# VectorE waits for the GpSimd instruction that precedes it on the shared port

## The chip, the cores and the metric

The kernel runs on one core of a Trainium2 chip. A core has five engines that work side by side[...]: TensorE (PE in the profile, its weight loads PEld) multiplies matrices, ScalarE (ACT) evaluates functions, VectorE (DVE) and GpSimd (POOL) do elementwise work, and SyncE (SP) issues transfers. The time is the device time of one execution in microseconds. Before the change it is 772.55 us, the median of three runs between 772.16 and 772.81.

## The reference

A gate mixes two branches over one input x of 2048 rows and 512 columns, all in bf16:

```
g = sigmoid((x * gate_w).sum(-1))
out = g * A(x) + (1 - g) * B(x)
```

A is attention with 32 heads of width 16: `softmax(q k^T / 4) v`, then a projection `wo`. The scores are 32 x 2048 x 2048 numbers, and each needs an exponential. B is a mixer: a layer norm, a projection `w1` with GELU, a shift of four column groups by one or two rows, a projection `w2` and a residual; then a layer norm, `w3` (to 1792 columns) with GELU, and `w4`, with a residual.

## The kernel before, in words

**Attention in rounds.** There are 32 rounds: four column blocks of 512 queries, by four groups of eight heads, by two halves of a group. A round takes 64 score tiles of 128 keys by 512 queries. TensorE computes a tile (L842) from `kT` and `q`. An exponential turns it into weights, and TensorE multiplies these with `V` and adds into the PSUM bank `acc` (L1017). `V` has a column of ones, so the sum of the weights comes with it.

**Two ways to the exponential.** Most tiles go to ScalarE in pairs: `PA<-psA`, 128x1024, L922. The others go to VectorE. There a trick on the bits of a 16-bit number stands for the exponential: a multiply and an add make an integer whose bits, read as bf16, approximate the power (L948, `PD<-ring`, one tile of 512 from a PSUM bank called `ring`). Two tiles make a pair of 1024 columns. Three shifted copies of the pair are then made by adding a constant to the integers (`close_pair`, L984 on VectorE, L986 on GpSimd, all of them `PD<-PD`, from SBUF to SBUF in 16 bits), and the four versions are added up by four products with `V`, or with `V2`, a scaled copy. VectorE makes the first copy, and mostly the second; GpSimd makes the third, and at times the second too. Pairs marked `alone` have all copies made by VectorE.

**Other work.** VectorE also casts the projections out of PSUM (L578, L601, L618, L733, L765), makes the masked copies of q (L603), scales `V` (L623), normalises rows for the layer norms (L688, L695), scales x by the gate (L753), empties `acc` at the end of each round (L1033), and multiplies the reciprocals of the sums with the gate (L1041). GpSimd also multiplies the emptied `acc` with the broadcast reciprocals (L1050) and computes the inverse deviations of the layer norm (L684, L686).

**Who sets the order.** No scheduler runs on the chip. When the kernel is built, a planner (`Sim`) plays through the whole execution with a cost for each job, and decides at each moment which job an engine takes next. The instructions are then emitted in the order of the planned start times, and each engine works its own list strictly in that order. Dependencies through data become semaphore waits.

**The shared port.** VectorE and GpSimd share a port to SBUF. The planner knows this: a job marked `port=True` (all of GpSimd's, and of VectorE's those that read SBUF in the ways concerned: L603, L623, L688, L695, L753, L984, L1041) starts in the plan only when `self.lock` has passed, that is, when the last such job of either engine is planned to be over (`try_engine`). The plan so has the port's jobs of both engines in one row. `in_port_order` makes the chip keep to that row, as far as it adds waits for it. Before the change it adds them on one side: a GpSimd instruction waits for the last VectorE port instruction that precedes it in the row (`last_port`). A VectorE port instruction has no such wait; it starts when its data and its buffers are there, and what happens on the port then is left to the hardware.

Of the kernel before, what the change touches and what calls it, by code (L numbers as in the profile page):

```python
# [89 lines left out]
class Sim:  # L90
# [50 lines left out]
    def in_port_order(self, e, fn):  # L141

        def issue():
            inst = fn()
            if e == "DVE":
                self.last_port = inst
            elif inst is not None and self.last_port is not None:
                self.tc.add_manual_dep(inst.ins, self.last_port.ins.name, mybir.DependencyInfo(
                    mybir.DependencyClass.Sync, mybir.DependencyReason.DATA), reason="port")
        return issue  # L150

    def finish_job(self, job):
# [93 lines left out]
def kernel(  # L246
# [89 lines left out]
    def slots(name, n, shape, dt=BF16, where=const):  # L336
        return [where.tile(shape, dt, name=f"{name}{i}") for i in range(n)]
# [38 lines left out]
    sim = Sim({  # L376
        **{f"psA{w}{n}": slots(f"psA{n}", 1, [P, 512 * w], F32, ps) for n, w in enumerate(WIDTHS)},
        "ring": sim_ring,
        "PA": slots("PA", NPA, [P, 512 * max(WIDTHS)]),
        "token": list(range((NPD - 1) // 3)),  # L380
        "PD": slots("PD", NPD, [P, 1024], U16),
        "w": slots("w", NW, [P, KT, D]),
        "xnT": slots("xnT", 2, [P, KT, 512]),
        "xn": slots("xn", 2, [P, D]),
# [11 lines left out]
        "rr": slots("rr", 3, [4, 512], F32, dpool),  # L396
    })
    sim.tc = tc
    sim.last_port = None

    def dve(hold, deps, fn, **kw):
        return sim.add(Job("DVE", hold, 280.0, deps, fn, **kw))
# [971 lines left out]
```

The softmax here doesn't subtract the row's maximum and nothing guards it: scores larger than these inputs give would overflow.

## Time and profile before

| what | value |
|---|---|
| time, median of 3 | 772.55 us |
| span of the profiled execution | 770.4 us |
| TensorE busy | 758.7 us, 98% |
| ScalarE busy | 739.7 us, 96% |
| VectorE busy | 725.2 us, 94%, 1575 instructions |
| GpSimd busy | 335.2 us, 44%, 332 instructions |
| one shifted copy on VectorE (L984, 128x1024) | 429 ns mean, 286 to 1262 ns, x579 |
| one shifted copy on GpSimd (L986, 128x1024) | 1048 ns mean, 1041 to 1215 ns, x270 |
| one tile's bits on VectorE (L948, 128x512) | 680 ns mean, x565 |

Busy time is the union of the stretches in which an engine executes something. A wait on a semaphore is not busy time: the engine is idle, and the profile names who released it. A wait inside an instruction that has started is different: the instruction simply takes longer, and shows only in its duration. Consecutive VectorE instructions overlap a little in the trace[...]. The ends of matmuls are modelled, so a busy TensorE is not TensorE at its peak.

### The profile page before, as it was taken

To read this page: it belongs to the slowest core of one execution; us is meant where nothing else is said; L and a number is where in the kernel's file an instruction comes from. 1 tells how busy PE (TensorE), PEld (TensorE's weight loads), DVE (VectorE), ACT (ScalarE), POOL (GpSimd) and SP (SyncE) were. 2 spreads that over 40 slices of the span, in tenths; PEclk is the share of its full clock that TensorE was granted. 3 is DMA by queue.
4 is the path that set the end of the run, shared out by engine and by line. 5 is a ranking of instruction groups with operands and counts; after the bars stand their busy time and mean duration, and the time that the engine had idled before them with its cause. 6 is when DMAs were issued, how large, how long until landed. Compare 5 with 4: busy or idle time off the path is not lost.

```text
span 770.4 us, 23725 instructions
## 1 busy us (share of the span) xinstructions
PE 758.7 (98%) x9588; PEld 227.8 (30%) x9588; DVE 725.2 (94%) x1575; ACT 739.7 (96%) x767; POOL 335.2 (44%) x332
## 2 busy tenths in 40 slices
PE   9999999999999999999999999999999999999997
PEld 5333322223222222233232224222233222223222
DVE  6999999999999999998989998999999889999996
ACT  6899999999999999999989999999999999999995
POOL 2345533443344444344345553344454454454531
PEclk9999999999999999999999999999999999999999
DMA  9402133122001221141001001001100000000001
GB/s 192 142 3 35 54 98 88 47 72 89 6 19 34 61 72 46 48 125 50 17 18 33 23 20 47 23 27 27 41 19 19 23 19 22 27 20 20 13 18 38
DMA packets 67093, 34.60 MB, mean 45 GB/s; under 512 B 46748, under 2 KB 62380, under 8 KB 66984
## 3 DMA queue, kind: packets, MB, share of 16 engines
q1 hardware_dynamic: 66040, 32.56, 16.3%
q8 instruction: 75, 1.23, 0.6%
q10 hardware_dynamic: 944, 0.52, 0.2%
q14 instruction: 34, 0.28, 0.1%
HBM read 17.40 MB, written 6.81 MB: 31 GB/s over the span
## 4 chain that ended last, share of the span: by engine, by line
PE 71%; ACT 22%; DVE 4%; issue 3%; ACTq 0%; DVEq 0%
PE acc L1017 26%; PE psA L842 23%; PE ring L532 20%; ACT PA L922 16%; DVE PD L948 2%; ACT hT L766 2%; ACT hB L766 2%; DVE PD L984 1%; ACT hT L735 1%; ACT L922 1%; PE ring L842 1%; PE ring L510 0%; ACT L766 0%; PE ring L1295 0%; DVE hB L765 0%
## 5 line engine op out<-in xcount | busy, mean ns | idle before, releaser
L922 ACT ACTIVATE PA<-psA 128x1024 bf16<-128x1024 f32 x742 | 689.8, 1052 | 16.8 <-PE acc L1017 7.7
L986 POOL TENSOR_SCALAR PD<-PD 128x1024 uint16<-128x1024 uint16 x270 | 281.8, 1048 | 384.7 <-DVE PD L984 215.8
L948 DVE TENSOR_SCALAR PD<-ring 128x512 uint16<-128x512 f32 x565 | 372.9, 680 | 25.9 <-PE ring L842 23.6
L1017 PE MATMUL acc<-PD,V 128*17 128x512 bf16 x2260 | 307.3, 381 | 1.0 <-DVE accsb L1033 0.8
L842 PE MATMUL psA<-q,kT 32*128 32x512 bf16 x1483 | 285.8, 384 | 5.3 <-ACT PA L922 4.4
L1017 PE MATMUL acc<-PA,V 128*17 128x512 bf16 x1483 | 277.6, 381 | 0.0
L984 DVE TENSOR_SCALAR PD<-PD 128x1024 uint16<-128x1024 uint16 x579 | 226.2, 429 | 1.5 <-PE acc L1017 0.8
L842 PE MATMUL ring<-q,kT 32*128 32x512 bf16 x565 | 190.7, 384 | 0.0
L842 PEld LDWEIGHTS <-kT 32*128 32x128 bf16 x2048 | 76.8, 91 | 311.0 <-issue 309.0
L1017 PEld LDWEIGHTS <-V 128*17 128x17 bf16 x3743 | 74.9, 88 | 129.1 <-issue 107.0
L532 PE MATMUL ring<-xnT,w 128*32 128x512 bf16 x1152 | 89.0, 382 | 0.0
L532 PE MATMUL ring<-w,hT 128*32 128x512 bf16 x704 | 58.5, 383 | 0.1
L532 PEld LDWEIGHTS <-w 128*32 128x32 bf16 x1920 | 45.2, 95 | 43.9 <-issue 30.3
L1050 POOL TENSOR_TENSOR oT<-accsb,bcs 128x512 bf16<-128x512 f32 x31 | 39.5, 1275 | 24.7 <-DVE PD L984 19.4
L532 PE MATMUL ring<-w,w 128*32 128x256 bf16 (+1 forms) x768 | 41.1, 311 | 0.0
L532 PE MATMUL ring<-w,hB 128*32 128x512 bf16 x448 | 36.0, 383 | 0.0
L1033 DVE COPY accsb<-acc 128x512 f32<-128x512 f32 x31 | 21.1, 681 | 1.1 <-PE acc L1017 1.0
L675 DVE BATCH_NORM_STATS2 st<-x_sb 128x6 f32<-128x512 bf16 x32 | 21.5, 678 | 0.0
L532 PE MATMUL ring<-w,wq 128*32 128x512 bf16 x256 | 21.2, 383 | 0.2 <-ACT w L561 0.2
L532 PEld LDWEIGHTS <-hT 128*32 128x32 bf16 x704 | 14.8, 95 | 20.3 <-issue 15.5
L765 DVE CAST hT<-ring 128x512 bf16<-128x512 f32 x28 | 18.8, 680 | 1.1 <-PE ring L532 0.9
L765 DVE CAST hB<-ring 128x512 bf16<-128x512 f32 x28 | 19.0, 682 | 0.9 <-PE ring L532 0.7
(93 smaller groups left out, 263.5 us busy)
## 6 DMA issues: line engine op xcount, KB each, us to landing
bcs<-rr SPq DMA_DIRECT2D x124, 64.0 KB
xn_dram<-xn SPq DMA_DIRECT2D x32, 128.0 KB
w<-in_B_w_dram SPq DMA_DIRECT2D x5, 512.0 KB
oD<-oT SPq DMA_DIRECT2D x124, 16.0 KB
w<-in_B_w_dram SPq DMA_DIRECT2D x4, 448.0 KB
out_dram<-ot SPq DMA_DIRECT2D x14, 128.0 KB
x_sb<-in_A_x_dram SPq DMA_DIRECT2D x3, 512.0 KB
w<-in_A_wqkv_dram SPq DMA_DIRECT2D x2, 256.0 KB
```

The costliest lines, as they stand in the source:

```text
L532: units.append([Op("col", j, lambda j=j, lf=lf, rf=rf, n0=n0, n1=n1, st=st, sp=sp: nc.tensor.matmul(get()[32 * j:32 * j + 32, n0:n1], lhsT ...
L675: a = dve(600, deps, lambda: nc.vector.bn_stats(out=sb.slot[:], in_=x_sb[:, t, :]), prio=6, at=at, acq=[sb])
L765: pre.append(evac(g, PSUM_NS, lambda ps, m=m: nc.vector.tensor_copy(out=h2()[:, m, :], in_=ps[:])))
L766: ge = act(93 + 427 * FT + 2600, pre, lambda: nc.scalar.activation(out=h2(), in_=h2(), func=ACT.Gelu_apprx_tanh), prio=0)
L842: o = Op("row", i, lambda: nc.tensor.matmul(dst(), lhsT=kT[G][32 * i:32 * i + 32, kt * P:(kt + 1) * P], rhs=qbuf[G, c].slot[32 * i:32 * i ...
L922: job = act(hold, ops, lambda: nc.scalar.activation(out=pb.slot[:, 0:n], in_=buf.slot[:, 0:n], func=ACT.Exp, scale=0.25), acq=[pb], frees= ...
L948: nc.vector.tensor_scalar(out=pr["buf"].slot[:, h * 512:(h + 1) * 512], in0=buf.slot[:], scalar1=BITS_MUL, scalar2=BITS_ADD, op0=ALU.mult, ...
L984: return nc.vector.tensor_scalar(out=d[k][:, 0:w], in0=d[0][:, 0:w], scalar1=float(SHIFT * k), scalar2=None, op0=ALU.add)
L986: return nc.gpsimd.tensor_scalar(out=d[k][:, 0:w], in0=d[0 if both else 2][:, 0:w], scalar1=1.0, scalar2=float(SHIFT * (k if both else 1)) ...
L1017: o = Op("col", i, lambda: nc.tensor.matmul(acc[32 * i:32 * i + DH + 1, :], lhsT=lhs(), rhs=rhs(), start=st, stop=True, tile_position=(0, ...
L1033: e = dve(PSUM_NS, round_ops[r], lambda: nc.vector.tensor_copy(out=ab.slot[:], in_=acc[:]), acq=[ab], prio=0)
L1050: n = gp(1250, d3, lambda: nc.gpsimd.tensor_tensor(out=ob.slot[:], in0=ab.slot[:], in1=bb.slot[:], op=ALU.mult), acq=[ob], frees=[ab, bb], ...
```

## The change

The wait is made mutual. `last_port` becomes a table that holds the last port instruction of each of the two engines. A GpSimd instruction waits, as before, for VectorE's last one in the planned row; a VectorE port instruction now waits in the same way for GpSimd's last one. Its purpose is that the port is taken in the planned order on both sides, so that a VectorE instruction neither overtakes a GpSimd one that is late nor starts while one is running.

```diff
     def in_port_order(self, e, fn):
 
         def issue():
-            inst = fn()
-            if e == "DVE":
-                self.last_port = inst
-            elif inst is not None and self.last_port is not None:
-                self.tc.add_manual_dep(inst.ins, self.last_port.ins.name, mybir.DependencyInfo(
+            inst, other = fn(), self.last_port.get("POOL" if e == "DVE" else "DVE")
+            if inst is None:
+                return
+            if other is not None:
+                self.tc.add_manual_dep(inst.ins, other.ins.name, mybir.DependencyInfo(
                     mybir.DependencyClass.Sync, mybir.DependencyReason.DATA), reason="port")
+            self.last_port[e] = inst
         return issue
...
-    sim.last_port = None
+    sim.last_port = {}
```

A job whose function returns nothing (two small set-up jobs of GpSimd) neither waits nor is recorded. The planner's costs, its parameters and its choices are not touched.

## The prediction

> **What bounds the kernel now.** I read the busy shares first, then the chain of work that ended last, then the idle time of each engine, and last the rows in time where VectorE and GpSimd meet.
>
> ```profile
> PE 758.7 (98%) x9588; PEld 227.8 (30%) x9588; DVE 725.2 (94%) x1575; ACT 739.7 (96%) x767; POOL 335.2 (44%) x332
> ...
> PE 71%; ACT 22%; DVE 4%; issue 3%; ACTq 0%; DVEq 0%
> ...
> L986 POOL TENSOR_SCALAR PD<-PD 128x1024 uint16<-128x1024 uint16 x270 | 281.8, 1048 | 384.7 <-DVE PD L984 215.8
> L948 DVE TENSOR_SCALAR PD<-ring 128x512 uint16<-128x512 f32 x565 | 372.9, 680 | 25.9 <-PE ring L842 23.6
> ...
> L984 DVE TENSOR_SCALAR PD<-PD 128x1024 uint16<-128x1024 uint16 x579 | 226.2, 429 | 1.5 <-PE acc L1017 0.8
> ```
>
> TensorE, ScalarE and VectorE are all nearly full; the chain runs through TensorE, so a delay on VectorE counts only when it reaches a matmul. GpSimd is 44% busy, and its idle time is mostly its own wait for VectorE. In the waits of VectorE, GpSimd does not appear at all; VectorE's longest wait is for score tiles from TensorE:
>
> ```profile
> DVE PD L948 <- PE ring L842: 23.6, 62, 1.1
> ```
>
> So today nothing on VectorE visibly waits for GpSimd. But L984 means 429 ns and its line's durations run from 286 through a median of 417 to 1262: some of it is a wait inside the instruction. Two stretches of the timeline show how the two engines meet (start us, duration us). First a meeting where the VectorE instruction starts early in the GpSimd one:
>
> ```profile
> 333.48 1.05 POOL L986 TENSOR_SCALAR PD<-PD 128x1024 uint16<-128x1024 uint16 x1 [2.34 <-DVE PD L984]
> ```
> ```profile
> 333.23 0.68 DVE L948 TENSOR_SCALAR PD<-ring 128x512 uint16<-128x512 f32 x1
> 333.95 1.18 DVE L984 TENSOR_SCALAR PD<-PD 128x1024 uint16<-128x1024 uint16 x2
> ```
>
> The first of the two L984 starts at 333.948, the GpSimd instruction ends at 334.523, and L984 ends at 334.802: it took 854 ns, and ended 279 ns after GpSimd. The second meeting is the common one:
>
> ```profile
> 387.69 1.05 POOL L986 TENSOR_SCALAR PD<-PD 128x1024 uint16<-128x1024 uint16 x1 [0.79 <-DVE PD L984]
> ```
> ```profile
> 388.66 0.41 DVE L984 TENSOR_SCALAR PD<-PD 128x1024 uint16<-128x1024 uint16 x1
> ```
>
> L984 starts 81 ns before GpSimd ends (388.737) and takes its ordinary 408 ns: overlapping the last 100 ns or so costs nothing now.
>
> **What the Trainium skill says.** "SBUF — State Buffer", section "Who interferes with whom": a VectorE instruction in a two-port mode, or with two SBUF inputs, and a GpSimd instruction exclude each other; the one that issues second blocks fully. The trace agrees in kind: all 21 blocked L984 among the new waits end 277 to 285 ns after that instruction's end. Not in the letter: the last 100 ns of overlap are free. "VectorE: DVE Perf Modes", section "The DRAIN you can't avoid", says a semaphore after each VectorE instruction cost nothing extra in its test. [...] in this trace VectorE instructions that wait for nothing start some 82 ns before the one in front ends, and that overlap goes when a wait is still open.
>
> **The change, part by part.** The planner's order does not move: the two programs have the same instructions in the same order on every engine. The cost model of the planner is untouched. What differs is which GpSimd instruction a VectorE instruction waits for. VectorE instructions with a wait on GpSimd go from 249 to 245, so nearly all is replaced, not added: waits for an old GpSimd instruction (a buffer coming free, 96 on L984 and 44 on L948) are covered by the new ones. I cost those at nothing in either direction, since none shows in VectorE's waits. Wait-only rows on VectorE's sequencer go from 243 to 282: 39 times the 21 ns median of such a row is 0.8 us, on a sequencer that runs ahead of an engine that is 94% busy; nothing, again.
>
> The cost is in the 244 VectorE instructions whose wait now asks for a later GpSimd instruction than anything asked for before. For each I took from the rows of the trace the end of that GpSimd instruction and the start of the VectorE one:
>
> - 152 start after GpSimd has ended. Free, except 7 that start less than 35 ns after it (below).
> - 65 start while it runs and take their ordinary time; together they start 4.9 us before its end, most of them 80 to 120 ns each.
> - 24 start while it runs and block on the port (21 of them L984, which end 277 to 285 ns after it).
> - 3 start before GpSimd has begun: they overtake it.
>
> The price of an open wait is the time from GpSimd's end to VectorE's start. No L984 shows it. The nearest row is L513, which waits for GpSimd's iota (L498):
>
> ```profile
> 1.45 0.14 POOL L498 IOTA mi<- 128x1 int32 x1
> ```
> ```profile
> 1.62 0.15 DVE L513 TENSOR_SCALAR mb<-mi 128x1 int32<-128x1 int32 x1
> ```
>
> End 1.588, start 1.623: 35 ns. L515 and L517, which wait for VectorE itself, also start 34 to 35 ns after. So 35 is the low end. The high end is the other way round, GpSimd waiting for VectorE: most often 155 ns. I take 35, because the waiter is VectorE, and keep 155 for the range.
>
> With 35 ns, the new end is GpSimd's end + 35 + the ordinary duration (416 for L984, 342 for L603, 185 for L1041, 398 for L695):
>
> - The 65 overlaps: 4.9 us of start time lost + 65 x 35 ns = 2.3, so 7.1 us.
> - The 24 blocked: GpSimd's end + 35 + 416 = 451 against 279 now, so some 172 ns each: 4.2 us.
> - The 3 overtakers: 2.9 us (at 81.69 us L984 would start 1.0 us later, at 526.58 us some 1.4 us net, at 103.3 us 0.5).
> - The near misses: 0.1 us.
>
> Sum: 14.2 us of added lateness on VectorE. With 155 ns the same sum is 27.6.
>
> What is queued behind: VectorE works in order, so behind the waiting L984 stand L948, which frees a score bank for TensorE, the casts of the projections, and accsb. Who waits for them is TensorE, and it is late only if lateness exceeds its margin. Of 1017 places where TensorE needs a VectorE result not asked for before, 23 start within 60 ns of that result (53 is the least, so they truly wait), 63 within 300, 106 within 400, 314 within 600, 719 within 1000. VectorE itself has 41.0 us of idle time in 143 gaps, which give lateness back where they are not themselves caused by a late TensorE. I carried the lateness down the rows of the trace with these facts: add each wait's delay, subtract the idle gap before the next instruction, let GpSimd be late by what its releasing L984 is late beyond its margin, and where lateness exceeds a TensorE margin, move the whole kernel by the excess, since TensorE at 98% has nothing to give back. The delay that reaches TensorE is 4.9 us with 35 ns, 6.3 with 60, 9.2 with 100, 14.6 with 155. TensorE's own waits for GpSimd were left out (a tenth of the 269 have a margin under 434 ns), so I round the first up to 5.5. Forecast: 772.55 + 5.5 = **778.0 us**.
>
> **The rivals.**
> 1. *Hidden.* The middle margins of TensorE's four largest groups are 550 to 1000 ns, each delay only 120 to 170 ns, so nothing arrives: 772.5. For: VectorE is 4% of the chain. Against: delays come in 98 places with 41 us of gaps between 143 places, and lateness piles up; 23 margins are zero already.
> 2. *All of it arrives.* VectorE at 94% plus 14.2 us is 739.4 of 770, as full as ScalarE: 772.55 + 14.2 = 786.8. The same time comes from a 155 ns wake with partial hiding (+14.6). For: 94% leaves few gaps. Against: half of TensorE's margins exceed 700 ns.
> 3. *Faster*, the other side: what the port costs now is won back. VectorE loses 9.8 us in 26 blocked instructions, but it works in order and would spend that time waiting on the semaphore instead; nothing queued behind may pass. What could be won is GpSimd's: 270 x (1048 - 1041) = 1.9 us if its instructions are stretched by VectorE, on an engine that is 44% busy. At best 770.6.
>
> **How the numbers follow.** Forecast (a part arrives, +1.6 to +10 us): 0.66. All arrives (beyond +10): 0.17. Hidden (within 1.5 us): 0.10. Faster by over 1.5 us: 0.07. So slower 0.83, same 0.10, faster 0.07. The range runs from 774.0, where little more than a tenth of the 14.2 arrives, to 787.0, which takes in the full sum and the 155 ns wake: it leaves out Hidden, Faster and a little above.
>
> **What would show it.** GpSimd should appear among VectorE's waits, with some 90 to 100 waits of L984 and others, 10 to 20 us in all. L984 should fall from 429 to about 415 ns mean with a maximum near 450, since nothing blocks inside any more. GpSimd's L986 should stay at 1048. TensorE's idle time and the share of VectorE in the chain should grow a little. VectorE's start after GpSimd's end should be 35 ns in open waits. The prediction is wrong if that wake is near 100 ns or more (then 782 to 787), if the idle time before L948 shrinks by as much as the new waits take (then hidden), or if TensorE's gaps to ScalarE soak up what I let run through.

## The result, and the profile after

The changed kernel takes 775.68 us (median, 775.28 to 775.98) against 772.36 us (771.96 to 772.81). The ratio is 1.0043, with a 95% interval of 1.0025 to 1.006: 3.3 us slower. (An amount in us with a sign is the ratio applied to the time of before; the difference of the medians can deviate from it by 0.2 us.) Apart from the rows that only wait, both programs have the same instructions in the same order on VectorE, so the traces can be laid on each other row by row.

The page of the kernel after (all lines moved down by one, so L984, L986 and L948 are now L985, L987 and L949):

```profile
PE 762.5 (98%) x9588; PEld 230.2 (30%) x9588; DVE 720.5 (93%) x1575; ACT 742.1 (96%) x767; POOL 333.4 (43%) x332
...
PE 62%; ACT 18%; DVE 11%; issue 4%; POOL 3%; DMA 1%; SPq 0%; POOLq 0%; ACTq 0%; DVEq 0%
...
L987 POOL TENSOR_SCALAR PD<-PD 128x1024 uint16<-128x1024 uint16 x270 | 280.9, 1045 | 387.2 <-DVE PD L985 222.5
L949 DVE TENSOR_SCALAR PD<-ring 128x512 uint16<-128x512 f32 x565 | 373.2, 684 | 18.5 <-PE ring L843 16.7
...
L985 DVE TENSOR_SCALAR PD<-PD 128x1024 uint16<-128x1024 uint16 x579 | 219.9, 420 | 16.8 <-POOL PD L987 11.8
```

Three things moved. In the chain, VectorE went from 4% to 11%, and GpSimd, which had no share, has 3%: the path that sets the end now runs through GpSimd into VectorE in places. The shifted copy on VectorE became shorter (429 to 420 ns), and its line's longest fell from 1262 to 434 ns: the waiting has left the instruction. And 16.8 us of idle time now stand in front of it, where there were 1.5. The waits of VectorE name the new releaser. They also show who paid in part: the idle time ahead of the tile's bits went from 25.9 to 18.5 us.

```profile
DVE PD L949 <- PE ring L843: 16.7, 45, 1.0
DVE PD L985 <- POOL PD L987: 11.8, 20, 2.1
...
DVE PD L985 <- POOL oT L1051: 1.3, 4, 0.7
DVE pk L1042 <- POOL PD L987: 1.2, 2, 0.7
```

Here is the first of the two meetings that the prediction showed, as it is now. GpSimd comes first, then VectorE (start and duration in us):

```profile
335.43 1.04 POOL L987 TENSOR_SCALAR PD<-PD 128x1024 uint16<-128x1024 uint16 x1 [2.27 <-DVE PD L985]
```
```profile
335.19 0.69 DVE L949 TENSOR_SCALAR PD<-ring 128x512 uint16<-128x512 f32 x1
336.51 0.43 DVE L985 TENSOR_SCALAR PD<-PD 128x1024 uint16<-128x1024 uint16 x1 [0.64 <-POOL PD L987]
```

VectorE stands idle for 0.64 us, starts 34 ns after GpSimd's end, and needs its whole time from there. Before, it had started at once, blocked, and ended 279 ns after GpSimd; now it ends some 460 ns after. The second meeting, the common one:

```profile
390.41 1.04 POOL L987 TENSOR_SCALAR PD<-PD 128x1024 uint16<-128x1024 uint16 x1 [0.95 <-DVE PD L985]
```
```profile
390.77 0.68 DVE L949 TENSOR_SCALAR PD<-ring 128x512 uint16<-128x512 f32 x1
391.49 0.43 DVE L985 TENSOR_SCALAR PD<-PD 128x1024 uint16<-128x1024 uint16 x1
```

Before, L984 started 81 ns ahead of GpSimd's end; now it starts some 34 ns behind it. No idle time is printed for it, because the gap after L949 is only about 40 ns: VectorE lost the overlap with its own instruction in front as well, and a view of idle time does not count that. This is why the list of waits understates the change: it has 29 waits for GpSimd, 15.3 us in all. By the rows of the trace, 116 of the 244 new waits are open, 114 of them with VectorE's start 33 to 36 ns after GpSimd's end; counted from the moment when the instruction in front would have let them start (82 ns before its end), these 114 held VectorE 26.6 us. The time that blocking on the port cost before is part of that.

One caution on durations. A tile's bits take 680 ns in before and 684 in after, with the same code. From the start of one to the start of the next, where they follow each other directly, it is 600 to 601 ns in both, and 599 to 601 in all the runs below. So only the recorded end moved; VectorE was not slower. It goes with the chip, where that is on record: 684 to 686 ns in the four runs on chip 4, 683 to 684 in the three on chip 7, 680 to 681 in the four on chip 11. An ordinary shifted copy has 3 to 5 ns more in the same runs (median 421 to 422 in after and on chip 4, 417 to 419 in before and on chip 11), so the means of 429 and 420 understate by as much how far the copies were relieved.

### The profile page after: what moved, and what is told of

It reads as the page before. It is cut to its first block, busy times and chain, and to the rows that moved or that the text cites. A ratio compares the mean times of both kernels' runs of the same rounds, so it can differ in the third digit from the quotient of the medians.

```text
span 774.2 us, 23763 instructions
## 1 busy us (share of the span) xinstructions
PE 762.5 (98%) x9588; PEld 230.2 (30%) x9588; DVE 720.5 (93%) x1575; ACT 742.1 (96%) x767; POOL 333.4 (43%) x332
## 3 DMA queue, kind: packets, MB, share of 16 engines
q1 hardware_dynamic: 66040, 32.56, 16.8%
## 4 chain that ended last, share of the span: by engine, by line
PE 62%; ACT 18%; DVE 11%; issue 4%; POOL 3%; DMA 1%; SPq 0%; POOLq 0%; ACTq 0%; DVEq 0%
PE acc L1018 22%; PE psA L843 20%; PE ring L533 18%; ACT PA L923 14%; DVE PD L985 4%; DVE PD L949 4%; POOL PD L987 3%; ACT hB L767 2%; ACT hT L736 1%; ACT hT L767 1%; DMA bcs<-rr 1%; ACT L923 1%; POOL oT L1051 1%; PE ring L843 1%; DVE st L676 0%
## 5 line engine op out<-in xcount | busy, mean ns | idle before, releaser
L923 ACT ACTIVATE PA<-psA 128x1024 bf16<-128x1024 f32 x742 | 692.2, 1049 | 17.8 <-PE acc L1018 7.7
L987 POOL TENSOR_SCALAR PD<-PD 128x1024 uint16<-128x1024 uint16 x270 | 280.9, 1045 | 387.2 <-DVE PD L985 222.5
L949 DVE TENSOR_SCALAR PD<-ring 128x512 uint16<-128x512 f32 x565 | 373.2, 684 | 18.5 <-PE ring L843 16.7
L985 DVE TENSOR_SCALAR PD<-PD 128x1024 uint16<-128x1024 uint16 x579 | 219.9, 420 | 16.8 <-POOL PD L987 11.8
L1018 PEld LDWEIGHTS <-V 128*17 128x17 bf16 x3743 | 76.5, 88 | 133.8 <-issue 111.2
```

The costliest lines, as they stand in the source:

```text
L923: job = act(hold, ops, lambda: nc.scalar.activation(out=pb.slot[:, 0:n], in_=buf.slot[:, 0:n], func=ACT.Exp, scale=0.25), acq=[pb], frees= ...
L949: nc.vector.tensor_scalar(out=pr["buf"].slot[:, h * 512:(h + 1) * 512], in0=buf.slot[:], scalar1=BITS_MUL, scalar2=BITS_ADD, op0=ALU.mult, ...
L985: return nc.vector.tensor_scalar(out=d[k][:, 0:w], in0=d[0][:, 0:w], scalar1=float(SHIFT * k), scalar2=None, op0=ALU.add)
L987: return nc.gpsimd.tensor_scalar(out=d[k][:, 0:w], in0=d[0 if both else 2][:, 0:w], scalar1=1.0, scalar2=float(SHIFT * (k if both else 1)) ...
L1018: o = Op("col", i, lambda: nc.tensor.matmul(acc[32 * i:32 * i + DH + 1, :], lhsT=lhs(), rhs=rhs(), start=st, stop=True, tile_position=(0, ...
```

## Experiments

The planned order makes it possible to put the new waits at chosen places. `WAITS` below is a set of numbers of VectorE's 710 port instructions; GpSimd's own waits stay. The places were sorted by what the trace of before shows there: `w_lap` has the 65 overlaps, `w_block` the 24 that blocked, `w_over` the 3 overtakers, and `w_done` the 152 where GpSimd had ended. These kernels have four lines more than before (L984 is L988 there, L986 is L990, L948 is L952).

```diff
-            if other is not None:
+            n = self.last_port["n"] = self.last_port.get("n", -1) + (e == "DVE")
+            if other is not None and (e == "POOL" or n in WAITS):
```

**Each kind of meeting alone.** Four kernels on one chip, with before at 772.29 us.

> VectorE waits for GpSimd only at the 65 places where, before, it started during the last part of the GpSimd instruction without being blocked. My theory (an open wait costs the lost overlap plus a 35 ns wake, 7.1 us on VectorE, part of which reaches TensorE): +1.4 us over before, at most +7. Order theory (the cost is the few places where VectorE used to overtake a late GpSimd instruction): 0. Overhead theory (each wait costs a little in the sequencer whether open or not): a quarter of the +3.3, +0.9.

Measured: 773.39 us, ratio 1.0011 (1.0003 to 1.0019), +0.9 us. This is below the +1.4 expected and within the interval (+0.2 to +1.5), but it is also just what the overhead theory gave; `w_done` has to separate the two.

> VectorE waits for GpSimd only at the 24 places where, before, it started and then blocked on the port. My theory (GpSimd's end + 35 + a whole instruction instead of GpSimd's end + 279, 4.2 us on VectorE): +1.2 us over before, at most +4. Order theory: 0, since the order is the same either way. Overhead theory: a tenth of the +3.3, +0.3. If a wait on the semaphore were no dearer than one on the port: 0.

Measured: 773.46 us, ratio 1.0015 (1.0009 to 1.0022), +1.2 us.

> VectorE waits for GpSimd only at the 3 places where, before, it started ahead of a GpSimd instruction that was planned in front of it. My theory (2.9 us on VectorE in three pieces of 0.5 to 1.4 us, each longer than TensorE's usual margin): +1.3 us over before. Order theory: all of the +3.3. Overhead theory: 0.

Measured: 772.46 us, ratio 1.0001 (0.9993 to 1.0009): no difference that can be measured, and at most 0.7 us, where +1.3 was expected. That expectation was missed.

> VectorE waits for GpSimd only at the 152 places where, before, the GpSimd instruction had ended when VectorE started. My theory: 0 within 0.5 us, since the waits are met. Order theory: 0. Overhead theory (a wait costs though it is met): most of the +3.3, about +2.

Measured: 772.51 us, ratio 1.0000 (0.9992 to 1.0008): none, and at most 0.6 us.

So 152 waits that are met cost nothing that can be measured, where the overhead theory (each wait costs, open or not) gave about 2 us; it is out. The 3 overtakers cost at most 0.7 us, where the order theory (the cost lies in places whose order changes) gave 3.3; it is out too. The waits that open a gap where there was overlap or a blocked instruction do cost, +0.9 and +1.2. For the blocking group the page shows how, in `w_block`:

```profile
L952 DVE TENSOR_SCALAR PD<-ring 128x512 uint16<-128x512 f32 x565 | 374.9, 686 | 23.8 <-PE ring L846 21.8
L988 DVE TENSOR_SCALAR PD<-PD 128x1024 uint16<-128x1024 uint16 x579 | 221.4, 423 | 11.2 <-POOL PD L990 8.7
```

The copies' recorded mean fell by 6 ns (429 to 423), or by some 11 if the later recorded ends of that chip are taken off (the median rose from 417 to 422): with 579 copies an estimated 6 us. The idle time ahead of them grew from 1.5 to 11.2 us: more than was saved.

Why the overtakers were free is seen at the largest of them. VectorE in the kernel before, and then in `w_over`:

```profile
526.58 2.43 DVE L984 TENSOR_SCALAR PD<-PD 128x1024 uint16<-128x1024 uint16 x3 [0.38 <-PE acc L1017]
```
```profile
528.21 1.10 DVE L988 TENSOR_SCALAR PD<-PD 128x1024 uint16<-128x1024 uint16 x3 [2.06 <-POOL PD L990]
```

The wait starts three copies 1.63 us later, but before they blocked on the port right after overtaking, one behind the other: they took 2.43 us, and now take 1.10. They end at 529.31 instead of 529.01. The other two were not followed in this way.

**The two costly groups together.**

> The waits at the 65 overlapping and the 24 blocking places together, without the 3 overtakers and the 152 that were met. Alone the two groups gave +0.9 and +1.2. If the groups add up and the overtakers count for little: +2.1 to +2.5. If the rest of the change's +3.3 comes from piling up between the two groups: +3. If it comes from the overtakers after all, in company with the others: +2, and the whole change then needs them.

Measured: 774.78 us against 772.55 us, ratio 1.0029 (1.0017 to 1.004), +2.2 us. The groups add up; the interval (+1.3 to +3.1) also overlaps that of the whole change (+1.9 to +4.6), so whether the met waits and the overtakers add anything in company is not settled. Nor is what the wait-only rows on VectorE's sequencer add: the whole change has 282 of them against 243 before, but `w_lap`, `w_block`, `w_done` and `w_lapblock` have only 211 to 227. So the costs of `w_lap`, `w_block` and `w_lapblock` don't come from more rows, but the 39 more of the whole change were never tried alone. In the trace of after, 261 of its rows were over more than 82 ns before the end of the instruction then running, which speaks against a cost.

**Few places or all.** By laying the matmuls of before and after on each other, one finds where TensorE falls behind for good. The first 0.33 us are there by 6.7 us, before VectorE has any port instruction (the first is at 13.05 us), so they are not the change's; the other traces differ there by up to 1 us. With these included, the lateness grows in steps: 0.8 us at 106 us, 1.25 at 187, 2.0 at 275, 2.3 from 359 to 398, 3.4 at 438, and then it is nearly flat until 3.75 at the end. Sixteen of the 244 waits stand just ahead of the steps. Two theories are at odds: a delay counts only where TensorE has no margin (margin theory), or each counts for about the same share (proportional theory).

> All new waits of the change but 16: those 16 just ahead of the places where TensorE fell behind in the trace of after. The 228 that stay make up 11.6 of the 14.2 us that the waits add to VectorE by the sum of the prediction. Margin theory (a delay counts only where it exceeds what TensorE has in hand, and such places are few): +0.3 us over before, at most +1. Proportional theory (VectorE is full, so each us added to it costs about the same share, 3.3 of 14.2): +2.7.

Measured: 773.27 us against 772.11 us, ratio 1.0015 (1.0007 to 1.0022), +1.2 us.

> Only those 16 waits, 2.6 of the 14.2 us on VectorE. Margin theory: +2.5 to +3 us over before, less what neighbours add by piling up. Proportional theory: +0.6.

Measured: 774.03 us, ratio 1.0023 (1.0015 to 1.0031), +1.8 us. Neither theory holds in full. The 16 waits have 18% of VectorE's added lateness (3.1 of 17.8 us in the trace of after), and they give 60% of the cost (0.0023 of 0.0023 + 0.0015): a delay does count mostly where TensorE has nothing in hand. But the other 228 cost more than the 0.3 us that the margin theory gave (its "at most +1" lies within the interval, +0.5 to +1.7). The trace of `w_butfew` shows where: TensorE falls behind by 0.4 us between 137 and 161 us, where it lost 0.13 in after. With the 16 gone, other places come to the front.

**A plan that knows when GpSimd really ends.** The planner reckons GpSimd's job from the moment when the port comes free. In the trace it starts 155 ns after VectorE's reported end, which itself lies 82 ns beyond VectorE's turn. That would explain why VectorE's next copy so often comes 80 to 120 ns too early. The next kernel keeps the port locked longer in the plan.

```diff
-            self.lock = self.t + j.hold
+            self.lock = self.t + j.hold + (270.0 if e == "POOL" else 0.0)
```

> The planner keeps the port locked 270 ns longer behind each GpSimd job (155 ns from VectorE's end to GpSimd's start, 82 of VectorE's overlap, 29 of a longer instruction: what the trace shows and the plan leaves out); waits on GpSimd's side alone, as before. The plan is another one, so its own time may fall or rise: theories give none, 765 to 785. L984 should hardly block any more, mean near 420 ns.

Measured: 819.40 us, ratio 1.061 (1.0596 to 1.0625). The time is far outside what I had allowed (765 to 785). L984 takes 420 ns on average, as expected, but one still took 1414. It is another plan, and a poorer one; probably its other settings fit the old lock, which was not tried. VectorE is 87% busy and ScalarE 91%, and VectorE waits twice as long for score tiles as before:

```profile
PE 785.4 (96%) x9727; PEld 243.2 (30%) x9727; DVE 713.2 (87%) x1554; ACT 746.0 (91%) x772; POOL 324.8 (40%) x324
...
DVE PD L948 <- PE ring L842: 47.2, 90, 2.6
```

As a kernel it is of no use; as a base for the comparison it serves.

> The same longer lock in the plan, with the waits on both sides. My theory (the waits cost because GpSimd ends later than the plan says, so that they are still open when VectorE comes): within 0.7 us of the kernel with the longer lock and waits on one side, since the waits are met. If the waits cost for another reason (their number, the added wait rows, the order): +3.3 against it, as without the longer lock.

Measured: 820.07 us, ratio 1.0616 (1.0601 to 1.063). On the longer lock the waits on VectorE's side make 0.0006 of the time of before, with intervals that overlap widely, against 0.0043 without it. (In these two kernels the granted clock was 0.983 to 0.990, and 1.0 in the others. At 0.990 both took 818 us: 818.21 and 818.00.) In `shift_both` little is left to wait for:

```profile
L985 DVE TENSOR_SCALAR PD<-PD 128x1024 uint16<-128x1024 uint16 x569 | 210.9, 416 | 7.6 <-PE acc L1018 2.7 <-POOL PD L987 2.2 <-POOL oT L1051 1.1
```

So the same waits are nearly free when the plan brings VectorE later than GpSimd's end. This kernel also has more slack on VectorE, which would hide part of a cost, so it supports the theory and does not prove it alone.

**GpSimd's side.** If an open wait is dearer than a blocked port, are GpSimd's waits worth having? The first kernel drops all waits for the port's order, the second only GpSimd's:

```diff
-            if other is not None:
+            if False:
...
-            if other is not None:
+            if other is not None and e == "DVE":
```

> No waits for the order of the port on either side: GpSimd too starts when its data are there. In the program 85 of its 332 instructions then wait for less; in the trace of before 74 of those start right behind the VectorE instruction they were made to wait for, a median 840 ns after the last one they need. My theory (the port blocks whoever comes second, and only VectorE's lateness counts): GpSimd takes the port ahead of VectorE's copies in a good part of the 74, each blocking VectorE by up to 1 us; slower than before, +2 to +10. If waits of any kind are the cost: faster than before, by 1 to 3 us.

Measured: 782.56 us against 772.55 us, ratio 1.0131 (1.0117 to 1.0145), +10.1 us, at the upper end of what was expected.

> VectorE waits for GpSimd as in the change, and GpSimd no longer waits for VectorE's port instructions. My theory: GpSimd runs ahead as above, but ends earlier too, so VectorE's waits are met more often and its port instructions block on later GpSimd instructions instead; between the change (+3.3) and +10 over before. If the cost lay in the two engines waiting for each other in turn: below the change, +1 or less.

Measured: 787.78 us, ratio 1.0194 (1.018 to 1.0208), +15.0 us: beyond what I had allowed. VectorE's copies, in `p_none` and then in `p_vector_only`:

```profile
L985 DVE TENSOR_SCALAR PD<-PD 128x1024 uint16<-128x1024 uint16 x579 | 240.6, 455 | 1.1 <-PE acc L1018 0.2
```
```profile
L985 DVE TENSOR_SCALAR PD<-PD 128x1024 uint16<-128x1024 uint16 x579 | 243.2, 460 | 6.8 <-POOL PD L987 2.6 <-POOL oT L1051 0.4 <-PE acc L1018 0.2
```

Without its waits GpSimd takes the port ahead of VectorE, and a copy takes 455 ns on average instead of 429. With VectorE's waits on top, VectorE first waits for the GpSimd instruction ahead of it (6.8 us of idle time before the copies, against 1.1), and then still blocks on the next one (460 ns, up to 1493). A wait on GpSimd's side lets the engine wait that is 44% busy and spares the full one; a wait on VectorE's side makes the full one wait. No version beat the kernel before.

## Why the prediction was right, and where its sizes were off

The forecast was 778.0 us, +5.5 over 772.55; measured +3.3. Direction and mechanism hold; terms of the sum do not all have the right size. It put VectorE's lateness too low and TensorE's share of it too high, and that the two partly cancelled was luck. What each new wait added to VectorE can be read by comparing its end with that of the instruction in front, in the two traces:

| meeting | places | predicted, us | in after, us |
|---|---|---|---|
| overlap | 65 | 7.1 | 8.4 |
| blocked | 24 | 4.2 | 5.1 |
| overtakers | 3 | 2.9 | 1.9 |
| met before | 152 | 0.1 | 2.4 |
| sum | 244 | 14.2 | 17.8 |

- **The wake of 35 ns: right.** 34 ns in most open waits. The choice of the low end rested on one row of the start of the kernel, whose waiter was also VectorE. It carried the forecast: with 155 ns the sum would have been 27.6 us instead of 14.2.
- **An open wait against an overlap: right in kind, a little small.** The prediction used 416 ns for L984; behind an open wait it takes 427 ns on average (94 of them), while copies in the same trace that start before the one in front has ended take 421. So 6 ns belong to the wait, and the rest to the later recorded ends. An overlap lost 129 ns on average (131 at the median) instead of the 109 of the sum.
- **Blocked: right for most.** It is 179 ns at the median, 172 predicted. The sum is 5.1 us instead of 4.2, because six of the 24 lost 202 to 413 ns; why these did was not traced.
- **Overtakers: too dear.** The sum took 1.0, 1.4 and 0.5 us; against the instruction in front their ends moved by 0.3, 1.2 and 0.4. Behind the largest the copies no longer block, and of its 1.2 us 0.3 is left two instructions later; alone, the group costs nothing that can be measured.
- **Waits met before: not free in company.** GpSimd waits for VectorE too, so when VectorE is late GpSimd's ends can move, and 25 of the 152 are open in after. Alone they cost nothing (ratio 1.0000).
- **What reaches TensorE: too much.** This is the term that put the forecast high: 4.9 of 14.2 us (35%), rounded up to 5.5, where 3.3 of 17.8 (19%) arrived. I let VectorE give back only its printed idle time, 41.0 us. But instructions that wait for nothing overlap by 82 ns, so a row with a gap of 0 has 82 ns in hand, and one with a gap of 100 has 182. With 80 ns counted for each, VectorE has 55.6 us to give back. Laid on each other, the two traces show that it used this: 17.8 us came in at the new waits and 2.2 at other instructions; 10.2 were given back out of printed idle time and 4.2 out of the 82 ns beyond it; 1.8 more were made up (0.8 by the copy behind the largest overtaker, which no longer blocked, the rest in differences of a few ns); 3.8 are left at VectorE's last instruction, 0.3 of which were there from the start. No run isolates this term. With it, the same carrying gives 3.6 us instead of 4.9, reckoned afterwards from the 14.2 predicted; from 17.8 it would give more, so that 3.6 comes near the 3.3 measured is no proof. The round-up for TensorE's waits on GpSimd was not needed.
- **Replaced waits and wait-only rows at nothing.** For the replaced waits `w_done` agrees. The 39 added rows were not tried alone, as said above.
- **The rivals.** Hidden is out by the interval (+1.9 to +4.6 against at most 1.5). All of it arriving is out. Faster is out: GpSimd's longest copy went from 1215 to 1054 ns, as that rival foresaw, and it bought nothing on an engine that is less than half busy. The mean went from 1048 to 1045 ns, but `w_done` has 1045 as well and is not faster, so that is not a gain of the change.
- **The signs.** L984 was to fall to about 415 ns with a maximum near 450 (420, 434); VectorE's waits for GpSimd were to be 90 to 100 with 10 to 20 us (29 with 15.3 us in the list, 116 by the rows). VectorE's share of the chain grew from 4% to 11%, more than the little that was foreseen. One sign failed: TensorE's idle time was to grow, and it is 11.8 us of the span before and 11.7 after; the longer time shows as busy time (758.7 to 762.5 us).

The Trainium skill, "SBUF — State Buffer", "Who interferes with whom", speaks of the second one as fully blocked. The trace agrees for VectorE's copies that meet more than the end of a GpSimd instruction. What matters here is the price: a blocked copy ends some 279 ns after GpSimd, one that waits on a semaphore some 34 + 427 ns after.

## What to carry to other kernels

A wait that only makes explicit an order which the chip keeps anyway is not free when it is open: here 131 ns at the median where the instructions had overlapped, and 179 where one had blocked. In this kernel it paid to put such waits on the engine with time to spare and to leave the full engine without: GpSimd's waits were worth 10 us, and VectorE's on top of them lost 3.3. When adding up what a delay costs downstream, count a full engine's slack from where the next instruction could have started, not from the end of the one in front; 4.2 us were given back there. And before reading a change of a few ns in a mean duration as an effect, look at the distance between starts.

## What the runs showed of the hardware

- The last part of a GpSimd instruction does not hold VectorE up. In before, 57 copies started with 118 ns or less of one left and took 407 to 421 ns. One that started with 151 ns left took 431. The limit is an estimate of 138 ns (416 - 278). The 24 copies that started with more than 150 ns of a shifted copy or of L1050 on GpSimd left ended 277 to 285 ns after it.
- Waking is not symmetric: VectorE starts 34 ns after GpSimd's end, GpSimd most often 155 to 156 ns after VectorE's.
- The recorded end of a VectorE instruction moved by 3 to 5 ns between chips, and the distance between starts did not: 684 to 686 ns against 680 to 681 for one tile's bits, 599 to 601 ns from one to the next in all.
